# A retention layer and a GELU MLP: four first loads on other queues, a new load order, and seven half-size products in block 0

## The chip, the core and the metric

The kernel runs on one core of one Trainium2 chip. The metric is the device time of one execution in microseconds; the time before is the median of three runs. A profile is one execution recorded by the hardware profiler, and every duration in this document comes from such a record or from the runs' times.

## What is computed

Batch 8, 8 heads, 576 positions, head dimension 64; then an MLP of 512 to 2048 to 512 features over 8 x 576 = 4608 tokens, with the heads side by side as the 512 features.

```python
scores = q @ k.T / sqrt(64)                       # per batch and head
ret    = scores * gamma[h] ** (i - j)             # for i >= j, else 0; gamma = 1 - 2 ** (-5 - h)
x      = (ret @ v) -> [4608, 512]                 # heads side by side
h      = x @ w_in                                 # [4608, 2048]
g      = 0.5 * h * (1 + erf(h / sqrt(2)))
out    = g @ w_out                                # [4608, 512], float32
```

## The kernel before

**Attention, in units.** The 576 positions of a batch are four chunks of 128 and a tail of 64. A unit is one chunk of one batch (or the tails of two batches), 128 tokens, 36 units in all; units are taken in pairs of batches, and a group is the unit or the two units that are handled together. Units 0 to 3 are the first chunks of batches 0 to 3. For each group TensorE transposes q and k (`turn`, L407, tile `qk_ps`; from group 8 on VectorE does it, L430), multiplies them to scores (`scores`, tile `sc`), VectorE multiplies the scores by a decay mask (`masked`, L507, tile `ret`; `near` for the first chunks, `msk` and `mskp` later) and v by a decay (`scaled_v`, L516, tile `vh`), TensorE multiplies the two (`inner`, tile `o_ps`). What earlier chunks contribute runs through a state of 64 x 64 per head: `state` (L557 and L562, tile `u_ps`) adds a chunk's k and v products, VectorE and ScalarE keep it in `u_acc` and `u_sb` (L567 to L577), and `cross` (L613) applies it. `evacuate` (L636, or L373 and L375 for units 0 to 3) writes x in bf16; `dqT` is the decay that it applies, built up by POOL (L280) from one chunk to the next.

**MLP, in blocks.** Four units make a block of 512 tokens, nine blocks. The first product (`mlp1`, L656, tile `hT`) has weight `w_in`, in eight slices of 256 columns; ScalarE applies GELU into `g_all` (L661, L664). The second product of block 0 is plain (`mlp2`, L689, tile `oT`, 512 columns a matmul, ScalarE copies the sum out, L693). The second product of blocks 1 to 8, in halves p of 256 tokens, is done by seven half-size products instead of eight (`mlp2_fast`, L760, tiles `fa` and `fb`, 256 columns a matmul). They need four sums of `g_all` for each half (`g_sum`, L728), and once for the whole kernel eight sums of `w_out` (`w_out_sums`, L715, into `wt` and, the last two, into `w_out` itself). The order of the seven is 1 2 6 5 7 4 3; product 6 needs the second sum of `wt`, 7 the one written over `w_out`. Their results are put together by copies (L373, L375, tile `t`) and VectorE additions (`join`, L746). Blocks 6 to 8 do the first product in the same way (L865, L878).

**Loads.** q and k of unit 0 come over SyncE's and ScalarE's queues as fp32 (L114) and are cast by `either` (L373 on VectorE or L375 on ScalarE, whichever the planner takes to be free sooner). Everything else that is loaded early comes over POOL's queue, which casts to bf16 on the way: q, k, v of a unit (128 KB written each, L315; into the tile `early` for units 0 to 3), the slices of `w_in` (`wi0` to `wi7`, L270) and of `w_out` (`wo0` to `wo7`, L285), 256 KB written each. Their order is a list written out by hand:

```python
321      ORDER = ("wi0 io v0 k1 q1 v1 wi1 q2 k2 v2 wi2 k3 q3 v3 wi3 wi4 wi5 wi6 wi7 wo0 wo1 wo2 wo3 wo4 wo5 wo6 wo7 "
322               "q4 k4 q5 k5 v4 v5 dq2 q6 k6 q7 k7 v6 v7 q8 k8 q9 k9 v8 v9 dq3 q10 k10 v10 dq4 q11 k11 q12 k12 n11 n12 dq0").split()
```

`io` makes the index ramps and the constants that hang on them (`near`, `dv`, `dqT`), `dq2` is a POOL multiplication for `dqT`. Later v comes over SyncE's queue (L261), later q and k over POOL's in small pieces (L298, L305). At most eight POOL loads are under way at a time.

**What sets the order.** All instructions are issued by a planner in the kernel, which runs when the kernel is built: it keeps a clock for each engine (`T`), a landing time for each load (`land`, with `sw` for the time up to which POOL's queue is taken), and picks what to issue next by these; it also puts matmuls on zeros (tile `warm`, L1080 and L1107) where TensorE would wait in the first 16 us. Each engine then runs its own list in that order, and waits where an operand isn't there. `either` chooses engines by the same clocks. The pieces that the change touches:

```python
1032         if sum_due and sum_ready(*sum_due[0]) <= now + 0.1:
1033             t, p, _ = sum_due[0]
1034             jobs.append(((t + 0.5 * p - b2) * PER_B, lambda: g_sum(*sum_due.pop(0))))
1035         if wsum and (wsum[0][0] != "3" or not left(runs2, 0)):
1036             jobs.append(((FAST2[0] - b2) * PER_B, lambda: wsum.pop(0)[1]()))
...
1135         for key in u_due[:1]:
1136             if key != (1, 0) or nA >= 6:
1137                 acts.append((state_at(*key), "U"))
```

The first lets VectorE make the sums of g and of `w_out` when it has nothing more urgent; the last holds back the state product of units 2 and 3.

Of the kernel before, what the change touches and what calls it, by code (L numbers as in the profile page):

```python
# [9 lines left out]
FP32 = mybir.dt.float32  # L10
# [7 lines left out]
def kernel(  # L18
# [14 lines left out]
    nc = tc.nc  # L33
    ctx.enter_context(tc.manual_schedule())

    B, H, S, D = q.shape
# [5 lines left out]
    C = 128  # L42
    N_DM = d_model // 128
    N_DF = d_ff // 128
# [22 lines left out]
    FAST2 = tuple(range(1, N_BLK))  # L67
# [3 lines left out]
    N_QKT = 4  # L71
# [4 lines left out]
    ALLOW = 0  # L76
    AHEAD = 14
    RATE = 3.8
    HOT = 7.5
    SLACK, SB, PER_G, PER_B, TURN0 = 1.6, 9.0, 8.0, 40.0, 3.0  # L80
    FINE = 0.38
# [9 lines left out]
    tr_pool = ctx.enter_context(tc.tile_pool(name="tr", bufs=1))  # L91
# [8 lines left out]
    T = dict.fromkeys(("pe", "act", "dve", "pool", "sp"), 0.0)  # L100
# [10 lines left out]
    first = {}  # L111
    for nm, src, eng in (("q32", q, nc.sync), ("k32", k, nc.scalar)):
        t = first[nm] = o_pool.tile([128, H, D], FP32, tag="o_sb", name=nm)
        eng.dma_start(t, src[0, :, 0:C, :].rearrange("h s d -> s h d"))  # L114
    zeros = ld_pool.tile([128, 512], BF16, tag="v32", bufs=N_V32, name="zeros")
    nc.vector.memset(zeros, 0.0)
    lgh = const.tile([128, H, 1], FP32, name="lgh")
# [91 lines left out]
            on(engine, dur)  # L209


    sw = [0.0]
    turned = [0.0]
    flying = []
    dq_done = {1}
    land = {}
    loaded = {}
# [17 lines left out]
    def tiles_of(i):  # L235
        g = groups[group_of[i]]
        if i not in loaded:
            if i < 4:
                loaded[i] = (early_slice(2 * i, 2).rearrange("p (a h d) -> p a h d", a=2, h=H),
                             early_slice(8 + i, 1).rearrange("p (h d) -> p h d", h=H), None)  # L240
            else:
                n = group_of[i]
                if i != g[0]:
                    qk, kn = loaded[i - 1][0], loaded[i - 1][2]
                elif n not in BY_DVE:
                    qk = qk_tile("qk_ld").rearrange("p (a h j d) -> p a h j d", a=2, h=H, j=2)
                    kn = qk[:, 1]
                else:
                    qk = qk_tile("qkb_ld").rearrange("p (a f) -> p a f", a=2)
                    kn = ld_pool.tile([128, H, 2, D], BF16, tag="kn", bufs=N_KN, name="kn_ld") if len(g) > 1 else None  # L250
                loaded[i] = (qk, None if group_of[i] in BY_DVE else ld_pool.tile([128, H, D], BF16, tag="v", bufs=8, name="v_ld"), kn)
        return loaded[i]
# [12 lines left out]
    def load(what, i):  # L265
# [43 lines left out]
        for jj in (j,) if j is not None else range(2):  # L309
# [3 lines left out]
            else:  # L313
# [2 lines left out]
            land[what, i] = sw_dma(0.88, 0.9) if j is not None else sw_dma(0.68, 0.5)  # L316

    tiles_of(0)
    land["q", 0], land["k", 0] = 4.65, 5.2
    cast_due = {("q", 0): (loaded[0][0][:, 0], first["q32"]), ("k", 0): (loaded[0][0][:, 1], first["k32"])}  # L320
    ORDER = ("wi0 io v0 k1 q1 v1 wi1 q2 k2 v2 wi2 k3 q3 v3 wi3 wi4 wi5 wi6 wi7 wo0 wo1 wo2 wo3 wo4 wo5 wo6 wo7 "
             "q4 k4 q5 k5 v4 v5 dq2 q6 k6 q7 k7 v6 v7 q8 k8 q9 k9 v8 v9 dq3 q10 k10 v10 dq4 q11 k11 q12 k12 n11 n12 dq0").split()

    def next_order():
        item = ORDER.pop(0)
# [603 lines left out]
    for t in range(N_BLK):  # L929
        if t in FAST1:  # L930
            for i in range(4):
                runs1.append((t, [("h", t, i, x) for x in "1265743"]))
        elif t < 2:
            for lo, hi in zip((0, 256), (256, 512)) if t else ():
                runs1.append((t, [("1", t, m, 2, lo, hi) for m in range(0, N_DF, 2)]))
            if t == 0:
                runs1 += [(t, [("1", t, m, 2, lo, lo + 128) for lo in range(0, TOK, 128)]) for m in range(0, N_DF, 2)]
        else:
            runs1.append((t, [("1", t, m, 1, 0, TOK) for m in range(N_DF)]))
        if t in FAST2:  # L940
            for p in range(2):
                runs2.append((t, [("f", t, p, x) for x in "1265743"]))
        elif t == 0:
            runs2.append((t, [("2", t, ts, m, m + 2) for m in range(0, N_DF, 2) for ts in range(2)]))
            runs2.append((t, [("2", t, ts, m, m + 4) for ts in range(2, 4) for m in range(0, N_DF, 4)]))
        else:
            runs2.append((t, [("2", t, ts, m, m + 4) for ts in range(4) for m in range(0, N_DF, 4)]))
    waiting2 = {x for _, r in runs1 + runs2 for x in r}
# [3 lines left out]
    def left(runs, t):  # L952
        return sum(len(r) for u, r in runs if u == t)
# [39 lines left out]
        return x_ready(t, 0, TOK)  # L993

    sum_due = []
    for t in FAST2:
        for p in range(2):
            sum_due += [(t, p, i) for i in "1234"]

    def done_step(t, p, name):  # L1000
        return ("f", t, p, name) not in waiting2

    def sum_ready(t, p, i):
        if i != "3" and t > FAST2[0] and not done_step(t - 1, p, {"1": "5", "2": "6", "4": "3"}[i]):
            return 1e9
        return max(g_at.get((t, m, ts), 1e9) for m in range(N_DF) for ts in (2 * p, 2 * p + 1))

# [11 lines left out]
    def side_jobs(now):  # L1019

        jobs = []
        gA, gB = group_of[min(nA, N_U - 1)], group_of[min(nB, N_U - 1)]
        b1, b2 = at_block(runs1, n1), at_block(runs2, n2)
        idle = T["dve"] <= now + SLACK
        if nV < min(N_U, len(s_done) + N_VH) and land.get(("v", nV), 1e9) + 0.1 <= now and (nV < nA or nV >= VH_POOL):
            if idle if nV < VH_POOL else T["pool"] <= now + 0.5:
                jobs.append(((group_of[nV] - gB) * PER_G + 1.0 + 9.0 * (nV in raw), do_vh))
        if not idle:
            return jobs
        if nT in BY_DVE and nT < gB + N_QKT and all(land.get(("qk"[half], i), 1e9) + 0.1 <= now for i in groups[nT]):  # L1030
            jobs.append(((nT - gA) * PER_G + TURN0, do_turn))
        if sum_due and sum_ready(*sum_due[0]) <= now + 0.1:
            t, p, _ = sum_due[0]
            jobs.append(((t + 0.5 * p - b2) * PER_B, lambda: g_sum(*sum_due.pop(0))))
        if wsum and (wsum[0][0] != "3" or not left(runs2, 0)):
            jobs.append(((FAST2[0] - b2) * PER_B, lambda: wsum.pop(0)[1]()))
        if wsum1 and len(s_done) >= N_U - ALLOW:
            jobs.append(((FAST1[0] - b1) * PER_B, lambda: wsum1.pop(0)[1]()))
        if xsum_due and xsum_ready(*xsum_due[0]) <= now + 0.1:
            jobs.append(((xsum_due[0][0] - b1) * PER_B, lambda: x_sum(*xsum_due.pop(0))))  # L1040
        return jobs
# [42 lines left out]
    def attend(n):  # L1084
        nonlocal nB
        g = groups[n]
        for i in g:
            inner(i)
            nB += 1
        if u_due and state_at(*u_due[0]) <= T["pe"] + 0.2 and not (u_due[0] == (1, 0) and nA < 6):  # L1090
            state(*u_due[0])
        cross(n)
        for i in g:
            evacuate(i)
# [15 lines left out]
    while True:  # L1110
# [22 lines left out]
                ready = max(ready, u_ready.get((bp, ci - 1), 1e9))  # L1133
            acts.append((max(ready, free_time(out_banks(g))), "A"))
        for key in u_due[:1]:
            if key != (1, 0) or nA >= 6:
                acts.append((state_at(*key), "U"))
        if nA < N_U:
            n = group_of[nA]
# [93 lines left out]
```

## Time and profile before

| | |
|---|---|
| runs, us | 300.9, 300.47, 300.14; median 300.47 |
| the profiled execution, us | 300.81 |
| its span, first to last instruction, us | 298.9 |
| granted TensorE clock, mean | 0.996 |
| TensorE (PE) busy | 286.1 us, 96% |
| VectorE (DVE) busy | 226.7 us, 76% |
| ScalarE (ACT) busy | 135.1 us, 45% |
| POOL busy | 152.9 us, 51% |
| DMA, POOL's queue | 17.71 MB in 78048 packets |
| DMA, SyncE's and ScalarE's queues | 16.26 MB in 32992 packets and 0.26 MB in 1040 |

How to read it: busy time is the share of the span in which an engine has an instruction in it, PEld is the loading of matmul weights, which runs beside matmuls. The filler matmuls on zeros count as busy. Rows of the timeline merge instructions of the same kind that follow each other closely; a bracket behind a row gives the idle time of its engine before it and what ended it. A few matmul records are missing from a trace, so a count of 35 can stand for 36.

### The profile page before, as it was taken

How to read it: one execution, taken by the hardware profiler on the slowest of the kernel's cores; microseconds unless marked ns; L12 is line 12 of the kernel's file. 1: busy time of each engine (PE TensorE's matmuls, PEld its weight loads, DVE VectorE, ACT ScalarE, POOL GpSimd, SP SyncE). 2: the span in 40 equal slices, each digit the busy share in tenths (PEclk: the TensorE clock that was granted, in tenths of full speed). 3: DMA queues.
4: the chain of work that ended last, by engine and by line, in shares of the span. 5: the costliest groups of instructions: out<-in, count | busy, mean ns of one | idle time of the engine just before them, and what ended most of it. 6: DMA issues, size and time to landing. Idle time of an engine off the chain costs nothing.

```text
span 298.9 us, 8793 instructions
## 1 busy us (share of the span) xinstructions
PE 286.1 (96%) x3689; PEld 213.8 (72%) x3718; DVE 226.7 (76%) x432; ACT 135.1 (45%) x262; POOL 152.9 (51%) x232
## 2 busy tenths in 40 slices
PE   7899997999999999999998999999999999999994
PEld 2478555888657656667665666666888888888883
DVE  5762059999999889317969489756998999898751
ACT  7656225744343343542542434433554554546421
POOL 8976797899896899996986842000000000000000
PEclk9999999999999999999999999999999999999998
DMA  9999999999999999999979570201001101111014
GB/s 143 166 186 204 182 187 179 214 163 113 155 141 197 189 201 125 155 162 159 139 126 174 83 188 2 72 2 37 35 2 72 71 2 70 44 28 72 35 55 124
DMA packets 112119, 34.79 MB, mean 116 GB/s; under 512 B 89808, under 2 KB 107728, under 8 KB 112080
## 3 DMA queue, kind: packets, MB, share of 16 engines
q0 software_dynamic: 78048, 17.71, 66.8%
q1 hardware_dynamic: 32992, 16.26, 20.2%
q8 instruction: 29, 0.48, 0.7%
q10 hardware_dynamic: 1040, 0.26, 0.4%
q14 instruction: 10, 0.08, 0.1%
HBM read 42.47 MB, written 9.44 MB: 174 GB/s over the span
## 4 chain that ended last, share of the span: by engine, by line
PE 62%; DMA 16%; POOL 16%; issue 3%; DVE 1%; ACT 0%; POOLq 0%; DVEq 0%; ACTq 0%
PE fa L760 17%; PE hT L656 14%; PE fb L760 13%; PE ha L865 7%; PE hb L865 5%; POOL qkb_ld L298 5%; DMA qkb_ld<-in_q_dram 3%; DMA qk_ld<-in_q_dram 3%; POOL kn_ld L305 3%; DMA kn_ld<-in_k_dram 3%; DMA w_out<-in_moe_w_out_dram 3%; POOL early L315 3%; DMA qk_ld<-in_k_dram 3%; PE sc L462 2%; POOL w_in L270 2%
## 5 line engine op out<-in xcount | busy, mean ns | idle before, releaser
L656 PE MATMUL hT<-x,w_in 128*128 128x512 bf16 (+2 forms) x521 | 92.6, 314 | 3.1 <-DVE x L636 1.0
L656 PEld LDWEIGHTS <-w_in 128*128 128x128 bf16 x544 | 49.1, 98 | 26.1 <-issue 3.2
L661 ACT ACTIVATE g_all<-hT 128x512 bf16<-128x512 f32 x64 | 38.2, 597 | 49.8 <-PE hT L656 47.6
L760 PEld LDWEIGHTS <-g_all 128*128 128x128 bf16 x512 | 49.6, 98 | 11.0 <-issue 0.2
L760 PEld LDWEIGHTS <-s 128*128 128x128 bf16 x384 | 37.4, 98 | 8.9 <-issue 0.2
L746 DVE TENSOR_TENSOR o_sb<-fb,t 128x256 f32<-128x256 f32 x48 | 19.9, 417 | 25.4 <-ACT t L375 12.9
L870 ACT ACTIVATE g_all<-tt 128x512 bf16<-128x512 f32 x36 | 22.6, 630 | 29.4 <-DVE tt L878 29.3
L298 POOL DMA_DIRECT2D qkb_ld<-in_k_dram x56 | 30.9, 587 | 6.5 <-DMA kn_ld<-in_k_dram 4.7
L760 PE MATMUL fa<-w_out,g_all 128*128 128x256 bf16 x256 | 33.1, 273 | 0.0
L305 POOL DMA_DIRECT2D kn_ld<-in_k_dram x44 | 30.4, 731 | 5.2 <-PE u_ps L557 2.3
L298 POOL DMA_DIRECT2D qkb_ld<-in_q_dram x56 | 31.3, 599 | 2.2 <-DMA qkb_ld<-in_k_dram 1.2
L507 DVE TENSOR_TENSOR ret<-sc,mskp 128x512 bf16<-128x512 f32 x44 | 27.2, 677 | 3.2 <-PE sc L462 3.1
L878 DVE TENSOR_TENSOR tt<-hb,tt 128x512 f32<-128x512 f32 x36 | 24.5, 687 | 5.2 <-ACT tt L375 2.9
L664 ACT ACTIVATE g_all<-hT 128x512 bf16<-128x512 f32 (+1 forms) x36 | 19.2, 550 | 14.2 <-PE hT L656 14.1
L375 ACT COPY t<-fa 128x256 f32<-128x256 f32 x35 | 13.0, 371 | 19.6 <-PE fa L760 19.6
L636 DVE TENSOR_TENSOR x<-o_ps,dqT 128x512 bf16<-128x512 f32 (+1 forms) x36 | 20.9, 619 | 0.8 <-PE o_ps L613 0.6
L865 PEld LDWEIGHTS <-ws 128*128 128x128 bf16 x192 | 18.8, 98 | 2.2
L516 POOL TENSOR_TENSOR vh<-v,dvp 128x512 bf16<-128x512 f32 x14 | 15.1, 1134 | 5.2 <-DMA v<-in_v_dram 5.2
L430 DVE STREAM_TRANSPOSE qkT<-qkb_ld 128x512 f32<-128x512 f32 (+1 forms) x28 | 17.4, 637 | 0.0
L760 PE MATMUL fb<-w_out,g_all 128*128 128x256 bf16 x128 | 16.6, 273 | 0.0
L760 PE MATMUL fb<-w_out,s 128*128 128x256 bf16 x128 | 16.4, 273 | 0.1
L760 PE MATMUL fa<-wt,g_all 128*128 128x256 bf16 x128 | 16.4, 273 | 0.0
(123 smaller groups left out, 445.2 us busy)
## 6 DMA issues: line engine op xcount, KB each, us to landing
out_dram<-o_sb SPq DMA_DIRECT2D x31, 256.0 KB, 2.8
v<-in_v_dram SPq DMA_DIRECT2D x50, 128.0 KB, 4.7
qkb_ld<-in_q_dram POOLq DMA_DIRECT2D x44, 64.0 KB, 3.6
qkb_ld<-in_k_dram POOLq DMA_DIRECT2D x44, 64.0 KB, 3.8
kn_ld<-in_k_dram POOLq DMA_DIRECT2D x44, 64.0 KB, 4.5
w_in<-in_moe_w_in_dram POOLq DMA_DIRECT2D x8, 256.0 KB, 7.1
w_out<-in_moe_w_out_dram POOLq DMA_DIRECT2D x8, 256.0 KB, 9.8
out_dram<-o_sb SPq DMA_DIRECT2D x8, 128.0 KB, 2.4
```

Source lines behind the costliest of these rows:

```text
L298: nc.gpsimd.dma_start(qk[p0:p0 + 32, "qk".index(what), 0:HP * per].rearrange("p (h x) -> p h x", h=HP), {"q": q, "k": k}[what][2 * bp + jj ...
L305: nc.gpsimd.dma_start(kn[64 * e:64 * e + 64, :, j], k[2 * bp + j, :, ci * C + e:ci * C + C:2, :].rearrange("h s d -> s h d"))
L507: nc.vector.tensor_tensor(r, t, by, op=ALU.mult)
L636: nc.vector.tensor_tensor(x[:, :, n * y:n * y + n], o, dqT[:, :, ci * C:ci * C + n], op=ALU.mult)
L656: nc.tensor.matmul(hT[:, m - m0, :], lhsT=w_in[:, cc, m * 128:m * 128 + 128], rhs=x_tiles[t][:, cc, lo:hi], start=(cc == 0), stop=(cc == N ...
L661: nc.scalar.activation(g_all[:, t % 2, :, m0, :], hT.rearrange("p n (a c) -> p (n a) c", a=2), AF.Gelu)
L664: nc.scalar.activation(g_of(t, 2 * lo // TOK)[:, m0:m0 + n, lo_:lo_ + hi - lo], hT, AF.Gelu)
L746: nc.vector.tensor_tensor(dst, src, f[key], op=ALU.add)
L760: nc.tensor.matmul(dst, lhsT=x[:, kk, :], rhs=y[:, kk, :], start=(name in "125" and kk == 0), stop=(kk == HK - 1), skip_group_check=True)
L865: nc.tensor.matmul(dst[:, m, :], lhsT=a[:, cc, c0:c0 + 128], rhs=y[:, cc, :], start=(name in "125" and m == 0 and cc == 0), stop=(cc == HC ...
L870: nc.scalar.activation(g_of(t, part)[:, m0:m0 + 2], src, AF.Gelu)
L878: nc.vector.tensor_tensor(f[key], f["b"][1], f[key], op=ALU.add)
```

## The change

Four more first loads (q and k of unit 1, v of units 0 and 1) come over SyncE's and ScalarE's queues as fp32, into two tiles of the pool `tr`, and are cast like the first two. They are taken out of POOL's list, which gets another order: the loads of units 2 and 3 stand among the first slices of `w_in`, slices of `w_in` and `w_out` are mixed and not in the order of their numbers, and q4 comes before the last slice. The second half of block 0's second product (tokens 256 to 511) is done by the seven half-size products, with its four sums of g; the sums of `w_out` may be made from when the plain part of block 0 is done. The state product of units 2 and 3 is held back until 24 us of the planner's clock instead of until six units have their scores. The planner's landing times are set for the new loads.

```diff
+    STATE10 = 24.0
+    HW_AT = 5.9, 6.4, 6.9, 7.5
...
+    for nm, src, i, eng in (("q1", q, 1, nc.sync), ("k1", k, 1, nc.scalar), ("v0", v, 0, nc.sync), ("v1", v, 1, nc.scalar)):
+        if len(first) % 2 == 0:
+            t = tr_pool.tile([128, 2, H, D], FP32, tag="qkT", bufs=N_QKT, name="first")
+        first[nm] = t[:, len(first) % 2]
+        eng.dma_start(first[nm], src[i, :, 0:C, :].rearrange("h s d -> s h d"))
...
-    sw = [0.0]
+    sw = [7.0]
...
+    tiles_of(1)
     land["q", 0], land["k", 0] = 4.65, 5.2
-    cast_due = {("q", 0): (loaded[0][0][:, 0], first["q32"]), ("k", 0): (loaded[0][0][:, 1], first["k32"])}
-    ORDER = ("wi0 io v0 k1 q1 v1 wi1 q2 k2 v2 wi2 k3 q3 v3 wi3 wi4 wi5 wi6 wi7 wo0 wo1 wo2 wo3 wo4 wo5 wo6 wo7 "
-             "q4 k4 q5 k5 v4 v5 dq2 q6 k6 q7 k7 v6 v7 q8 k8 q9 k9 v8 v9 dq3 q10 k10 v10 dq4 q11 k11 q12 k12 n11 n12 dq0").split()
+    land["q", 1], land["k", 1], land["v", 0], land["v", 1] = HW_AT
+    cast_due = {("q", 0): (loaded[0][0][:, 0], first["q32"]), ("k", 0): (loaded[0][0][:, 1], first["k32"]),
+                ("q", 1): (loaded[1][0][:, 0], first["q1"]), ("k", 1): (loaded[1][0][:, 1], first["k1"]), ("v", 0): (loaded[0][1], first["v0"]), ("v", 1): (loaded[1][1], first["v1"])}
+    ORDER = ("q2 io k2 v2 wi1 wi2 q3 wi0 k3 wi4 wo0 v3 wi5 wo4 wi7 wi6 wo1 wo2 wi3 wo3 wo6 wo5 q4 wo7 q5 k4 k5 q6 "
+             "v5 q7 v4 k6 k7 k8 q8 q9 k9 v9 dq2 q10 v8 v7 v6 dq3 q11 n11 dq0 k10 v10 k12 k11 q12 n12 dq4").split()
...
         elif t == 0:
             runs2.append((t, [("2", t, ts, m, m + 2) for m in range(0, N_DF, 2) for ts in range(2)]))
-            runs2.append((t, [("2", t, ts, m, m + 4) for ts in range(2, 4) for m in range(0, N_DF, 4)]))
+            runs2.append((t, [("f", t, 1, x) for x in "1265743"]))
...
-    for t in FAST2:
-        for p in range(2):
+    for t in (0, *FAST2):
+        for p in range(2) if t else (1,):
             sum_due += [(t, p, i) for i in "1234"]
...
-        if i != "3" and t > FAST2[0] and not done_step(t - 1, p, {"1": "5", "2": "6", "4": "3"}[i]):
+        if i != "3" and t and not done_step(t - 1, p, {"1": "5", "2": "6", "4": "3"}[i]):
...
-        if wsum and (wsum[0][0] != "3" or not left(runs2, 0)):
-            jobs.append(((FAST2[0] - b2) * PER_B, lambda: wsum.pop(0)[1]()))
+        if wsum and (wsum[0][0] != "3" or not any(r and r[0][0] == "2" for _, r in runs2)):
+            jobs.append(((0.5 - b2) * PER_B, lambda: wsum.pop(0)[1]()))
...
-            if key != (1, 0) or nA >= 6:
+            if key != (1, 0) or now > STATE10:
```

How the planner places it, in the order of each engine's instructions: VectorE casts q1, k1 and v1 and ScalarE v0, all ahead of the first mask (`near`). TensorE has 11 filler matmuls instead of 22, 32 `oT` matmuls instead of 64, 56 more of the half-size kind; six of the `oT` matmuls stand among block 0's `hT`, the other 26 behind it. On VectorE the four sums of g and then the eight sums of `w_out` stand ahead of the first `msk` masks (units 4 and 5); before, the eight stood between the masks and x of units 4 to 9. TensorE's products of block 0's second half stand between transposes and scores of units 4 to 7, and ahead of block 1's `hT`. POOL's `dq2` comes after v9.

More of the change, by code (lines that the diff above doesn't have):

```diff
@@ L1089, in attend @@
             nB += 1
-        if u_due and state_at(*u_due[0]) <= T["pe"] + 0.2 and not (u_due[0] == (1, 0) and nA < 6):
+        if u_due and state_at(*u_due[0]) <= T["pe"] + 0.2 and not (u_due[0] == (1, 0) and T["pe"] <= STATE10):
             state(*u_due[0])
```

## Prediction

> **What bounds the kernel now.** First the page: span, busy line, slices.
>
> ```profile
> span 298.9 us, 8793 instructions
> ...
> PE 286.1 (96%) x3689; PEld 213.8 (72%) x3718; DVE 226.7 (76%) x432; ACT 135.1 (45%) x262; POOL 152.9 (51%) x232
> ...
> PE   7899997999999999999998999999999999999994
> DVE  5762059999999889317969489756998999898751
> ```
>
> A slice is 7.5 us. TensorE is full from the eighth (52 us) on, less so before. VectorE has a hole in slices 4 to 6, then nines. Next the busy time by stretch (start:end, length, PE, PEld, DVE, ACT, POOL, granted clock, DMA share, GB/s):
>
> ```profile
> 6.00:8.00 2.00, 1.73 (x19) 0.98 (x18) 1.58 (x7) 1.48 (x5) 2.00 (x4) 1.00 2.37 154
> 14.00:16.00 2.00, 1.84 (x36) 1.38 (x34) 1.07 (x2) 1.16 (x3) 2.00 (x4) 1.00 2.21 162
> 28.00:32.00 4.00, 3.95 (x48) 3.52 (x48) 0.00 (x0) 3.08 (x7) 2.77 (x4) 1.00 1.24 204
> 48.00:52.00 4.00, 3.04 (x56) 1.82 (x50) 4.00 (x8) 1.10 (x2) 2.78 (x5) 1.00 2.32 188
> ```
>
> About 155 GB/s move where q, k and v run in short rows, 205 where weight slices do: the loads are the limit of the first stretch. At 28 to 32 VectorE does nothing; at 48 to 52 it is full and TensorE is not. The timeline (start, length, instruction, idle before it) shows who waits:
>
> ```profile
> 9.61 0.40 PE L407 MATMUL qk_ps<-ident,early 128*128 128x128 bf16 x4 [0.58 <-DMA early<-in_q_dram]
> 20.12 2.37 PE L656 MATMUL hT<-x,w_in 128*128 128x256 bf16 x24 [0.38 <-DMA w_in<-in_moe_w_in_dram]
> 31.55 7.93 PE L689 MATMUL oT<-w_out,g_all 128*128 128x512 bf16 x35
> 39.74 1.09 DVE L373 COPY qkT<-qk_ps 128x512 bf16<-128x512 bf16 x3 [15.05 <-PE qk_ps L407]
> 41.77 2.48 DVE L507 TENSOR_TENSOR ret<-sc,msk 128x512 bf16<-128x512 f32 x4 [0.93 <-PE sc L480]
> 44.77 2.71 DVE L516 TENSOR_TENSOR vh<-v_ld,dv 128x512 bf16<-128x512 bf16 x2
> 47.41 1.28 DVE L715 TENSOR_TENSOR wt<-w_out 128x1024 bf16<-128x1024 bf16 x2
> 50.41 1.27 DVE L636 TENSOR_TENSOR x<-o_ps,dqT 128x512 bf16<-128x512 f32 x2
> 51.74 1.03 PE L656 MATMUL hT<-x,w_in 128*128 128x256 bf16 x8 [0.81 <-DVE x L636]
> ```
>
> Three stages: loads, until block 0's first product (hT) ends at 31.55; then block 0's second product (oT) beside two attention groups, until VectorE's x releases block 1's first product at 51.74; then TensorE, which alone is on the chain of waits from 107 us to its last rows, of which this is one (start, length, what):
>
> ```profile
> 289.35 3.49 PE fa L760 x32
> ```
>
> So a microsecond won before 51.74 should be kept, as long as later loads keep up.
>
> **Work taken off TensorE.** Thirty-two oT matmuls go (35 in 31.55 to 39.10, 0.216 each: 6.9) and 56 half-size ones come (3.49/32 = 0.109 each: 6.1): -0.8. Of hT, 16 of 256 columns become 32 of 128, the same columns: 0. Eleven of 22 filler matmuls on zeros go; they only fill waits: 0.
>
> **The loads.** Four 256 KB loads leave POOL for the SyncE and ScalarE queues. One q, k or v load costs 0.87 and a weight slice 1.29: POOL's issues (L315) from 26.43 on come 1.28 apart, one as each slice lands, and about 0.9 apart from 34.71. Landing is then 3.95 plus the sum of the loads before it: q1's 9.60 is 3.95 + five small + one slice; q2, by the same count 12.64, was waited for until 12.69. I assume that the DMA engines give a byte the same time from either queue. Before, they were fed by SyncE and ScalarE until about 4 us and by POOL after, without a gap, so the new queues bring no bytes, only another order. The Trainium skill says the same in "Trainium Kernel Development and Optimization", Key Constraints: issuing from several engines saves only issue time; by that rule the queue move by itself is worth nothing here, as in my sum.
>
> By the new order x of units 0 to 2 needs nine small loads first (11.8, the fp32 ones earlier, about 10), the first w_in slice lands at 13.1, and the last, w_in 3, twelve small loads and twelve slices on: 3.95 + 10.4 + 15.5 = 29.9. Its 16 products take 1.75, and I allow 0.5 for TensorE running behind, about its two waits shown above: hT ends at 32.2 (31.7 if it is not behind). That is 0.6 later than before; but six oT matmuls are done by then, and the last w_out slice lands at 35.9, before the last four oT need it at 37.0.
>
> The loads of units 4 to 7 come just in time: by the same count q5 lands at 36.8 for transposes at 37.8, k5 at 38.5 for 40.0, k7 at 43.7 for 44.5, v4 at 42.0 for a vh at 44.1. A load that is later than this margin (0.8 to 2) costs its excess one for one.
>
> The other instructions: ScalarE issues two more DMAs (0.49 each) ahead of its table load, so near ends 1.0 later, at 6.6, and the first mask, 7.77 before, comes later anyway. SyncE issues two; nothing is behind them until the first store at 38.8. Four casts come: q1, k1, v1 on VectorE ahead of the first mask, v0 on ScalarE, 0.43 to 0.58 each. The first mask thus waits for v1, near 10.2 instead of 7.77; hidden, because the first w_in slice is not there until 13.1.
>
> **Block 0's second half.** Four sums of g (L728, 0.68) and the eight sums of w_out (L715) now stand together on VectorE after the last gelu, in its hole, ahead of the first msk masks. VectorE starts such instructions 0.60 apart (41.77 to 44.17 for four). From hT's end: gelu 0.85 (33.05), four dependent sums 2.5 (35.55), eight 4.8 (40.35), a join and a copy 0.75 (41.1), scores to mask 0.6, four masks 2.4 (44.1), two vh, two joins, a copy 2.3 (46.4). TensorE meanwhile has 5.6 of oT, 6.1 of products, 1.8 of transposes and 0.5 of scores: 46.2 without a wait; o_ps, u_ps, u_acc and two x follow to 49.35. Block 1's first product starts there, 2.4 before 51.74. The state product of units 2 and 3 (STATE10; 32 small matmuls at 41.72 and VectorE's copy at 44.17) has moved into hT, off this chain; its 0.6 is part of the 2.4. TensorE has also done 16 transposes more by then (48 instead of 32; 16 take 0.9, 44.67 to 45.56): 3.3 ahead in all, which contains the -0.8.
>
> One charge: the two vh at 44.77 took 2.71 instead of 1.28, while POOL multiplied dqT at 45.83. One such multiplication (dq2), which fell in VectorE's hole, comes near 41 now. It costs 0 if it meets an instruction that reads PSUM (the masks at 52 kept 0.62 beside one) and 1.4 if it meets a sum or vh: I take 0.5. After 51.74 VectorE is 4.8 lighter up to 57, where TensorE's gaps add to 0.1: 0.
>
> Sum: 3.3 - 0.5 = 2.8. The profiled execution took 300.81 (span 298.9 plus 1.9), 0.3 above the median: 298.0 against it, 297.7 against 300.47.
>
> **Rivals.**
> *Loads ahead of the count.* If the two fp32 queues fill the start (246 GB/s at 2 to 4 us, against 154 later), all lands up to 1.0 earlier and dq2 misses: 2.8 + 1.0 + 0.5, 296.2.
>
> *The lead is lost to the fp32 loads.* For it: v in 128 KB pieces on SyncE took 4.7 to land beside POOL's loads, the first 256 KB q only 3.8 alone. If v1 lands at 12.5 instead of 10, masks, x and hT move 2.5: 0.3 is left, 300.2. "DMA: Bandwidth & Descriptors", Queues, rings and completion order, in the Trainium skill has each DMA engine go round-robin over the queues, by packets; no row here shows three queues at once, and by it v1 would land near 10.
>
> *Slower.* The same place, further on: nothing of VectorE passes the cast of v1. Gain is zero at a first mask at 13.0 (10.2 + 2.8); v1 landing at 13.8 with k2 and wi1 waiting behind it puts hT's end at 36 and costs 1.0: 301.5. Against it: both queues start at 0.74, before POOL's first packets.
>
> *A cold TensorE.* At the start 512-column fillers take 0.64 (seven in 4.45) and later 0.25 (six in 1.47), though the granted clock reads 1.00. With half the fillers gone TensorE could fall back near 10 us. The slow pace lasted some 5 us at the start; 5 us of it hold 2.5 of work, so 2.5 is lost, of which waits for loads take up 1.0: 1.5, 299.2. The Trainium skill's "TensorE: Matmul & The Clock Gate", What's actually happening, has such a fallback after an idle window; no wait in my count is that long.
>
> **Numbers.** Forecast 0.48, loads ahead 0.16, lead lost 0.16, cold 0.05, slower 0.15. A measurement here tells 0.3% (0.9 us) from nothing. Faster: forecast, loads ahead, cold and 0.03 of lead lost, 0.72; same 0.13; slower 0.15. Time 297.7; range 295.9 (loads ahead, with 0.3 for a lighter VectorE) to 300.5 (lead lost).
>
> **What would show it.** Right: w_in 3 landing near 30, hT of block 0 ending near 32, twelve sums on VectorE from 33 to 40, block 1's first product near 49.4, no new idle on TensorE after 60. Wrong: the cast of v1 waiting past 12; a gap on TensorE after oT for wt or qkT; transposes (L430) waiting for qkb_ld between 60 and 110, which would mean that TensorE's lead outran POOL's loads.

## The result: 0.8% slower

| | runs | median, us | ratio to before, 95% interval |
|---|---|---|---|
| before, same session | 4 | 300.34 (300.14 to 300.9) | |
| after | 4 | 302.62 (302.33 to 303.68) | 1.0079 (1.0051 to 1.0108) |

The forecast was 297.7 with a range of 295.9 to 300.5. Single executions scatter more in the later sessions (the kernel before took 298.9 to 303.65 in one of them), so verdicts below are ratios over 6 to 35 executions of a session; the profile of one kernel, `e10_plain`, fell into a disturbed execution and is not read.

The profiled execution took 302.59, span 300.8. Lines of the code are ten higher than before (L656 is L666). The page of the kernel after, span, busy line and slices of TensorE and VectorE:

```profile
span 300.8 us, 8906 instructions
...
PE 287.7 (96%) x3747; PEld 216.9 (72%) x3747; DVE 227.6 (76%) x439; ACT 138.3 (46%) x270; POOL 150.0 (50%) x228
...
PE   7679999999999999999998999999999999999994
DVE  5564097989998899426968559865998999899751
```

TensorE's seventh slice is full now, as the change means it to be; its second and third are emptier than before (7 6 7 for 7 8 9). The busy time by stretch shows where, in the columns of the prediction:

```profile
8.00:10.00 2.00, 1.90 (x20) 1.46 (x20) 0.80 (x3) 1.56 (x5) 1.28 (x2) 1.00 1.53 184
10.00:12.00 2.00, 0.21 (x3) 0.00 (x0) 0.00 (x0) 0.55 (x2) 0.00 (x0) 1.00 1.84 159
20.00:24.00 4.00, 2.73 (x42) 2.63 (x42) 0.42 (x1) 3.99 (x12) 1.65 (x3) 1.00 1.59 191
48.00:52.00 4.00, 3.98 (x46) 3.35 (x45) 3.63 (x8) 1.96 (x5) 4.00 (x4) 1.00 2.15 188
```

From 10 to 12 the engines all but stand (TensorE 0.21, ScalarE 0.55, the others 0); from 20 to 24 TensorE is short of work while ScalarE is full. At 48 to 52 TensorE is full, where before it had 3.04 of 4. The timeline names the waits:

```profile
12.11 0.61 PE L417 MATMUL qk_ps<-ident,early 128*128 128x128 bf16 x4 [1.89 <-DMA early<-in_k_dram]
12.37 0.43 DVE L383 CAST early<-first 128x512 bf16<-128x512 f32 x1 [3.43 <-DMA first<-in_v_dram]
13.05 1.28 DVE L517 TENSOR_TENSOR ret<-sc,near 128x512 bf16<-128x512 f32 x2
18.64 0.33 ACT L206 ACTIVATE dvp<-dvp,ln_scale 128x40 f32<-128x40 f32 x1 [3.05 <-DVE dvp L200]
18.98 1.28 ACT L207 ACT_TABLE_LOAD   x1
20.64 0.58 ACT L385 CAST x<-o_ps 128x512 bf16<-128x512 f32 x1
21.27 1.93 PE L666 MATMUL hT<-x,w_in 128*128 128x128 bf16 x24 [1.68 <-ACT x L385]
35.58 1.91 PE L666 MATMUL hT<-x,w_in 128*128 128x256 bf16 x16
47.15 2.48 DVE L517 TENSOR_TENSOR ret<-sc,msk 128x512 bf16<-128x512 f32 x4 [0.89 <-PE sc L490]
54.85 1.91 PE L666 MATMUL hT<-x,w_in 128*128 128x256 bf16 x16
```

VectorE waits 3.43 for v1, which lands at 12.35; the first mask starts at 13.05 instead of 7.77. Then ScalarE waits 3.05 for `dvp`, whose small VectorE instructions (17.84 to 18.61) stand behind three pairs of masks, loads a table, and only then casts x of unit 1, though its product `o_ps` was done at 17.8. From 21.27 on TensorE has no gap worth naming before 54.85.

Three landmarks split the time. Block 0's hT ends at 37.49 (35.58 + 1.91) instead of 31.72: 5.8 later. From there to block 1's first product it takes 17.36 instead of 20.02: 2.7 won. From that product to the end of the span 245.95 instead of 247.16: 1.2 won, of which the sixteen transposes done earlier can be 0.9. 5.8 - 2.7 - 1.2 = 1.9, the difference of the spans.

### The profile page after: what moved, and what is told of

Same layout as the page of the kernel before. It is cut to its first block, busy times and chain, and to the rows that moved or that the text cites. A ratio compares the mean times of both kernels' runs of the same rounds, so it can differ in the third digit from the quotient of the medians.

```text
span 300.8 us, 8906 instructions
## 1 busy us (share of the span) xinstructions
PE 287.7 (96%) x3747; PEld 216.9 (72%) x3747; DVE 227.6 (76%) x439; ACT 138.3 (46%) x270; POOL 150.0 (50%) x228
## 4 chain that ended last, share of the span: by engine, by line
PE 82%; DMA 6%; DVE 4%; POOL 4%; issue 1%; ACT 1%; DVEq 0%; POOLq 0%
PE hT L666 23%; PE fa L770 19%; PE fb L770 14%; PE ha L875 7%; PE hb L875 5%; DMA early<-in_k_dram 3%; PE sc L472 3%; PE o_ps L623 3%; PE o_ps L552 2%; PE oT L699 2%; DMA qk_ld<-in_k_dram 2%; DVE ret L517 2%; PE u_ps L567 1%; POOL kn_ld L312 1%; DMA qkb_ld<-in_q_dram 1%
## 5 line engine op out<-in xcount | busy, mean ns | idle before, releaser
L666 PE MATMUL hT<-x,w_in 128*128 128x512 bf16 (+2 forms) x560 | 94.0, 314 | 2.9 <-ACT x L385 1.7
L666 PEld LDWEIGHTS <-w_in 128*128 128x128 bf16 x560 | 50.3, 98 | 27.0 <-issue 3.8
L770 PEld LDWEIGHTS <-g_all 128*128 128x128 bf16 x544 | 52.6, 98 | 11.7 <-issue 0.7
L770 PEld LDWEIGHTS <-s 128*128 128x128 bf16 x408 | 39.1, 98 | 9.3 <-issue 1.2
L756 DVE TENSOR_TENSOR o_sb<-fb,t 128x256 f32<-128x256 f32 x51 | 21.3, 419 | 23.2 <-PE fb L770 12.8
L770 PE MATMUL fa<-w_out,g_all 128*128 128x256 bf16 x272 | 35.1, 273 | 0.0
L385 ACT COPY t<-fa 128x256 f32<-128x256 f32 x38 | 14.2, 373 | 26.2 <-PE fa L770 25.2
L770 PE MATMUL fa<-wt,s 128*128 128x256 bf16 x136 | 17.5, 273 | 0.2 <-DVE s L738 0.2
L770 PE MATMUL fb<-w_out,s 128*128 128x256 bf16 x136 | 17.5, 273 | 0.1
L770 PE MATMUL fa<-wt,g_all 128*128 128x256 bf16 x136 | 17.5, 273 | 0.1
## 6 DMA issues: line engine op xcount, KB each, us to landing
w_out<-in_moe_w_out_dram POOLq DMA_DIRECT2D x8, 256.0 KB, 10.2
```

The source lines that it names most:

```text
L666: nc.tensor.matmul(hT[:, m - m0, :], lhsT=w_in[:, cc, m * 128:m * 128 + 128], rhs=x_tiles[t][:, cc, lo:hi], start=(cc == 0), stop=(cc == N ...
L756: nc.vector.tensor_tensor(dst, src, f[key], op=ALU.add)
L770: nc.tensor.matmul(dst, lhsT=x[:, kk, :], rhs=y[:, kk, :], start=(name in "125" and kk == 0), stop=(kk == HK - 1), skip_group_check=True)
```

## Experiments

Each was timed in five rounds beside the kernel before. Landmarks are from one profiled execution each. "Stage 2" is the time from hT's end to block 1's first product. "Measured" gives medians over all executions; the ratios decide.

| kernel | first mask | hT of block 0 ends | block 1's first product | stage 2 | ratio to before, 95% interval |
|---|---|---|---|---|---|
| before | 7.77 | 31.72 | 51.74 | 20.02 | 1 |
| after | 13.05 | 37.49 | 54.85 | 17.36 | 1.0079 (1.0051 to 1.0108) |
| e1_loads | 12.61 | 37.05 | 55.34 | 18.29 | 1.0033 (1.0021 to 1.0044) |
| e2_products | 8.29 | 32.05 | 62.14 | 30.09 | 1.0179 (1.0151 to 1.0206) |
| e3_skew | 12.84 | 36.00 | 53.36 | 17.36 | 1.0027 (1.0007 to 1.0046) |
| e4_pool | 7.95 | 34.13 | 52.78 | 18.65 | 0.9994 (0.9971 to 1.0017) |
| e5_products_state | 7.95 | 32.44 | 50.96 | 18.52 | 1.0041 (1.0004 to 1.0078) |
| e6_pool_skew | 7.97 | 33.95 | 52.62 | 18.67 | 0.9988 (0.9956 to 1.0021) |
| e7_pool_k10 | 7.95 | 35.68 | 53.05 | 17.37 | 1.0020 (0.9989 to 1.0051) |
| e8_pool_skew_k10 | 7.97 | 33.39 | 51.99 | 18.60 | 0.9964 (0.9941 to 0.9987) |
| e9_hw_skew_k10 | 13.29 | 36.44 | 53.81 | 17.37 | 1.0033 (1.0001 to 1.0066) |
| e10_plain | | | | | 1.0065 (1.0035 to 1.0096) |
| e11_k6k7 | 7.95 | 33.68 | 52.32 | 18.64 | 1.0010 (0.9974 to 1.0047) |
| e12_two | 8.78 | 35.77 | 53.14 | 17.37 | 0.9999 (0.9963 to 1.0034) |

Behind block 1's first product the profiled executions (e2 and e10 aside) take 244.5 to 248.0 to the end of the span, in no order that follows the landmarks. So a landmark tells where a microsecond goes, not what the time will be.

**e1_loads: the loads alone.**

```diff
-            runs2.append((t, [("f", t, 1, x) for x in "1265743"]))
+            runs2.append((t, [("2", t, ts, m, m + 4) for ts in range(2, 4) for m in range(0, N_DF, 4)]))
...
-        if wsum and (wsum[0][0] != "3" or not any(r and r[0][0] == "2" for _, r in runs2)):
+        if wsum and (wsum[0][0] != "3" or not left(runs2, 0)):
```

> The loads alone: four loads over the SyncE and ScalarE queues and the new order of loads, with block 0's second half as before (plain oT products). Theory: the loads are what costs, and the seven products gain behind them what was reckoned. In the kernel after, hT of block 0 ended 5.8 later than before and block 1's first product began 3.1 later, so the second half gave back 2.7; without it 302.6 + 2.7 = 305.3, hT of block 0 ending at 37.3 as in the kernel after. Rival: the products gain nothing (the time after a late hT shrinks by itself, since VectorE has more done by then): 302.6, the same as after.

Measured 301.55 against 300.80. The loads alone reproduce the late hT (37.05, the same order on TensorE as in the kernel after up to there), so the loss is theirs; e1 keeps the new place of the state product, too. That the whole would be 2.7 worse without the products was wrong: block 1's first product moved by 0.5 only, and the end came out better than after. Stage 2 had already shrunk from 20.02 to 18.29 without the products, since the state product and some oT had moved ahead of hT's end (30.84, 26.36 and 34.71).

**e2_products: the products alone.**

```diff
-        if u_due and state_at(*u_due[0]) <= T["pe"] + 0.2 and not (u_due[0] == (1, 0) and T["pe"] <= STATE10):
+        if u_due and state_at(*u_due[0]) <= T["pe"] + 0.2 and not (u_due[0] == (1, 0) and nA < 6):
...
-            if key != (1, 0) or now > STATE10:
+            if key != (1, 0) or nA >= 6:
```

The four loads are back on POOL's queue, too, and the list of loads is that of the kernel before.

> The products alone: block 0's second half by seven half-size products with its twelve sums on VectorE, loads and their order as before. Theory: the second half gains what it gave back in the kernel after, 2.7: 297.6, with hT of block 0 ending at 31.6 and block 1's first product starting near 49. Rival: the twelve sums only find room on VectorE because the new order of loads and the other place of the state product made it; with the old ones block 1's first product stays at 51 to 52: 299.8 to 300.5.

Measured 305.89. Both missed. The planner lets the sums of `w_out` begin only when the states of units 0 to 3 are done; with `nA < 6` back, that is near 44.5, and the sums stand among the masks. TensorE waits 0.92, 0.94 and 1.37 between 43 and 47.4, and then this (busy time by stretch, the eighth figure is the granted clock):

```profile
44.00:46.00 2.00, 1.04 (x9) 0.78 (x8) 2.00 (x5) 0.76 (x2) 1.95 (x3) 0.71 1.75 222
46.00:48.00 2.00, 0.65 (x12) 0.51 (x14) 2.00 (x2) 1.79 (x4) 1.79 (x2) 0.50 1.74 159
48.00:50.00 2.00, 2.00 (x16) 1.34 (x13) 2.00 (x5) 0.00 (x0) 0.62 (x1) 0.50 2.37 155
```

The granted clock falls to half; eight matmuls of 256 columns take 1.89 (48.38) instead of 1.04. The products need the third part of the change, the state product inside hT.

**e3_skew: ScalarE's order.**

```diff
         make_args()
+        make_skewed()
...
         for hp in range(HP):
             make_dq(hp)
+        make_dvp()
...
-    later = [(6.4, "dve", 0.65, make_skewed), (7.3, "act", 1.8, make_dvp), (MSK_AT, "dve", 1.4, make_msk)]
+    later = [(6.4, "dve", 0.65, lambda: None), (7.3, "act", 1.8, lambda: None), (MSK_AT, "dve", 1.4, make_msk)]
```

> The kernel after, with one thing moved: VectorE's four small skew instructions and ScalarE's dvp and its table load for gelu (L200, L206, L207 of the kernel after) stand ahead of the casts and masks instead of behind three pairs of masks. Nothing else changes its place. Theory B (ScalarE's order): x of unit 1 waits 2.8 on ScalarE behind dvp, which waits for VectorE; without that it comes at 18.4 instead of 20.6, hT of block 0 ends about 2.2 earlier: 300.4. Theory A alone (late loads make the first mask late, and everything else follows): x of unit 1 would have come no sooner, 302.6. Cost at most 0.65 on VectorE ahead of the first casts, 303.2 if that is on the path.

Measured 301.96 against 300.80: 0.5% better than after by the ratios, 1.6 us. TensorE's 24 matmuls follow without the wait of 1.68:

```profile
19.76 1.94 PE L668 MATMUL hT<-x,w_in 128*128 128x128 bf16 x24
...
62.99 0.39 PE L419 MATMUL qk_ps<-ident,qk_ld 64*128 64x64 bf16 x8 [1.29 <-DMA qk_ld<-in_k_dram]
```

Theory B holds, though hT ends 1.5 earlier and not 2.2. The second line is new: a transpose of unit 10 waits 1.29 for its k, where the kernel after waited 0.22. Loads later on take back part of what is won.

**e4_pool: the queues undone, the order kept.**

```diff
-    for nm, src, i, eng in (("q1", q, 1, nc.sync), ("k1", k, 1, nc.scalar), ("v0", v, 0, nc.sync), ("v1", v, 1, nc.scalar)):
...
-    sw = [7.0]
+    sw = [0.0]
...
-    ORDER = ("q2 io k2 v2 wi1 wi2 q3 wi0 k3 wi4 wo0 v3 wi5 wo4 wi7 wi6 wo1 wo2 wi3 wo3 wo6 wo5 q4 wo7 q5 k4 k5 q6 "
+    ORDER = ("q1 io k1 v0 v1 q2 k2 v2 wi1 wi2 q3 wi0 k3 wi4 wo0 v3 wi5 wo4 wi7 wi6 wo1 wo2 wi3 wo3 wo6 wo5 q4 wo7 q5 k4 k5 q6 "
```

> The kernel after, with q1, k1, v0 and v1 back on POOL's queue, at the head of the same order; ScalarE and SyncE issue only q0 and k0 early. The planner places ScalarE's and VectorE's early instructions anew. Theory A (two fp32 queues beside POOL's slow all three): with one queue v1 lands near 9.2 and v2 near 11.8 instead of 12.35 and 12.84, the first mask comes near 10 instead of 13.05, hT of block 0 ends 32 to 34: 297.5 to 299.5. Theory C (the order of the loads costs, w_in 3 being last): hT of block 0 ends at 36 or later whatever the queue, 301.5 to 303.

Measured 300.93 against 300.80, ratio 0.9994: 0.85% better than after. v1 lands at 9.17, k2 at 10.97 and v2 at 11.80, in the order of issue; in the kernel after they land at 12.35, 12.06 and 12.84, together. The first mask starts at 7.95, since it no longer stands behind the cast of v1. The queue lines of the DMA view show the queues at work, first the kernel after at 9 to 11 (packets, MB, share; q0 is POOL's queue, q10 ScalarE's, q1 SyncE's):

```profile
q0 software_dynamic: 767, 0.10, 73.9%
q10 hardware_dynamic: 772, 0.20, 67.6%
q1 hardware_dynamic: 169, 0.04, 16.0%
```

and a kernel with POOL's queue alone, `e8_pool_skew_k10` at 5 to 7:

```profile
q0 software_dynamic: 2328, 0.29, 230.1%
```

A packet is one row of 64 numbers in either case (0.29 MB / 2328 = 125 bytes as bf16, 0.20 MB / 772 = 259 as fp32). In these two stretches POOL's queue alone moves 1164 rows per us, all queues together 854; over 4 to 10 it is 6678 rows in e4_pool and 5583 in the kernel after, 1113 and 931 per us. POOL's queue also starts later: in the kernel after it has no packet before 5.5, though its first load was issued at 1.25. At 9 to 11 POOL's and ScalarE's queues got the same number, 767 and 772, so there each load waits for the other's; from 6 to 7 the shares were not equal (POOL's 310, ScalarE's 547, SyncE's 42). The rule of the Trainium skill in "DMA: Bandwidth & Descriptors", Queues, rings and completion order, that an engine goes round-robin over the queues by packets, agrees with the counts at 9 to 11 and not with those at 6 to 7; what the prediction concluded from it, v1 near 10, did not come.

Theory A holds: hT ends 3.4 earlier (34.13) and the time falls by 2.5, though 300.9 is short of the 299.5 that it promised at most. Theory C, with hT's end at 36 or later whatever the queue, falls.

**e5_products_state: the products and the state product, with the old loads.** e2_products with STATE10 back in both conditions.

```diff
-        if u_due and state_at(*u_due[0]) <= T["pe"] + 0.2 and not (u_due[0] == (1, 0) and nA < 6):
+        if u_due and state_at(*u_due[0]) <= T["pe"] + 0.2 and not (u_due[0] == (1, 0) and T["pe"] <= STATE10):
...
-            if key != (1, 0) or nA >= 6:
+            if key != (1, 0) or now > STATE10:
```

> The products alone once more, with the third part of the change that the second half needs: the state product of units 2 and 3 moved into hT (STATE10), loads and their order as in the kernel before. In e2_products the sums of w_out waited for that state product and stood among the masks (45 to 53 us), TensorE idled and its granted clock fell to 0.50 there. Theory (the change's second half is worth what the kernel after showed behind its late hT, and only the loads undid it): the twelve sums stand together ahead of the first msk masks, no clock below 1.0; the stretch from 20 to 60 us loses 1.2 less than before and TensorE has 0.7 less work: 300.8 - 1.9 = 298.9, and 298.0 if the prediction's own 2.8 holds. Rival (an earlier start of block 1 meets loads of q and k that are not there): the gain is lost at transposes between 55 and 70, 300.5.

Measured 301.17 against 300.66. The sums stand together and the clock stays at 1.00, but block 1 starts only 0.8 earlier, and the rival's waits are there (timeline):

```profile
50.50 0.62 PE L408 MATMUL qk_ps<-ident,qk_ld 128*128 128x128 bf16 x8 [0.70 <-DMA qk_ld<-in_q_dram]
57.63 0.58 PE L408 MATMUL qk_ps<-ident,qk_ld 64*128 64x64 bf16 x8 [0.62 <-DMA qk_ld<-in_k_dram]
65.65 0.59 PE L463 MATMUL sc<-qkT 32*128 32x128 bf16 x20 [1.23 <-DVE qkT L431]
```

The last wait is for VectorE's transposes, which themselves wait for the k load (`kn_ld`) at 63.7 and 64.9. TensorE had 0.8 more in hand and met loads that were no earlier.

**e6, e7, e8: the early win, the late k load, and both.** On e4_pool; e6 with the edit of e3_skew, e7 with this, e8 with both:

```diff
-             "v5 q7 v4 k6 k7 k8 q8 q9 k9 v9 dq2 q10 v8 v7 v6 dq3 q11 n11 dq0 k10 v10 k12 k11 q12 n12 dq4").split()
+             "v5 q7 v4 k6 k7 k8 q8 q9 k9 v9 dq2 q10 v8 v7 v6 k10 v10 dq3 q11 n11 dq0 k12 k11 q12 n12 dq4").split()
```

> e4_pool with the skew instructions and ScalarE's dvp and table load early, as in e3_skew. In e4_pool x of unit 1 still waited 1.4 on ScalarE; this takes that away, so hT of block 0 ends about 1.4 earlier (near 32.5). Theory (the late k load of unit 10, issued at 55 and landed at 62.4, sets the time at which TensorE may go on at 62.5, whatever came before): time the same as e4_pool, 300.9, with the wait for qk_ld grown from 1.4 to near 2.8. Rival (a microsecond won early is kept, as the prediction has it): 299.5.

> e4_pool with two loads moved in the order: k10 and v10 stand right behind v6, ahead of dq3, q11, n11 and dq0, as they did in the kernel before. Theory (the late k10 costs 1.4 at 62 us): the wait for qk_ld there goes, 300.9 - 1.4 = 299.5. Rival (the loads as a whole are late there, so that another one is waited for instead): 300.9.

> Both edits, of e6_pool_skew and of e7_pool_k10, at once. If the early win of 1.4 is lost at k10 and k10 itself costs 1.4, the two together gain 2.8 where the first alone gains nothing: 298.1. If the loads as a whole limit the stretch up to 65 us: 299.5 to 300.9.

Measured 300.16, 301.32 and 299.58 against 300.66. e6 gained nothing that can be told, as its theory said, but not at unit 10: the wait for x was gone and hT still ended only 0.2 earlier, because its last slice was not there:

```profile
32.03 1.92 PE L661 MATMUL hT<-x,w_in 128*128 128x256 bf16 x16 [0.73 <-DMA w_in<-in_moe_w_in_dram]
```

w_in 3 landed at 31.98. The wait at unit 10 did not grow (1.1). In e7 the wait at unit 10 is gone, and nothing was won. Its profiled execution lost 1.6 up to hT's end to a fall of the granted clock (last section), in a stretch where its program is that of e4, and waited 2.2 for a join at 155, which e4's did not. Only both together are faster than before, by 0.36%, interval 0.13 to 0.59; that is 1.1 us, the expectation's second branch (299.5 to 300.9) and not its first (298.1). That it takes both is not shown: in 7 of e6's 12 executions the mean granted clock was 0.997 or more and their median is 299.81, beside 299.58 for e8, whose 12 were all at 0.997 or more; in e6's other five it was 0.993 or 0.994 and the median is 302.35. In e8 the next wait stands in stage 2:

```profile
46.11 0.41 DVE L751 TENSOR_TENSOR o_sb<-fb,t 128x256 f32<-128x256 f32 x1
...
46.61 0.61 PE L412 MATMUL qk_ps<-ident,qk_ld 128*128 128x128 bf16 x8 [1.25 <-DVE o_sb L751]
```

The line blames VectorE's join, which ended at 46.52. But k7 landed at 46.48; either could be it.

**e11_k6k7: which of the two.** e8 with k6 and k7 ahead of v5 and v4.

```diff
-             "v5 q7 v4 k6 k7 k8 q8 q9 k9 v9 dq2 q10 v8 v7 v6 k10 v10 dq3 q11 n11 dq0 k12 k11 q12 n12 dq4").split()
+             "k6 q7 k7 v4 v5 k8 q8 q9 k9 v9 dq2 q10 v8 v7 v6 k10 v10 dq3 q11 n11 dq0 k12 k11 q12 n12 dq4").split()
```

> e8_pool_skew_k10 with k6 and k7 ahead of v5 and v4 in the order of loads (q6 k6 q7 k7 v4 v5). In e8_pool_skew_k10 the transposes of unit 7 waited 1.4 at 45 to 46.6; k7 lands at 46.5 to 47.3 in all kernels with the new order of loads, 2.8 later than the prediction's ledger had it. Theory (that load sets the time): the wait goes, 299.6 - 1.4 = 298.2. Rival (VectorE sets it: four masks, a vh and two joins stand one behind the other from 43.6 to 47, and the transposes wait for the bank that the join empties): 299.6, the wait unchanged.

The transposes did not wait (44.62). But the planner also put them one product earlier in TensorE's list, ahead of that join, so this run does not tell the load from the join. Nor do the others: the join ended at 47.24, 47.12 and 46.52 in e4, e6 and e8, and k7 landed at 47.27, 47.11 and 46.48. Either alone would have held the transposes as long. The time did not follow: ratio 1.0010. The last of v4 and v5 now lands at 47.0, x comes later, and the wait is one step on:

```profile
52.32 1.03 PE L661 MATMUL hT<-x,w_in 128*128 128x256 bf16 x8 [1.06 <-DVE x L641]
```

Block 1's first product comes at 52.3, in e8 at 52.0. This order did not help; no other was tried.

**e9_hw_skew_k10 and e12_two: the queues again, four loads and two, with both mends.** e9 is e3_skew with the order of e7; e12 is e9 with v0 and v1 on POOL's queue (`"v0 io v1 q2 k2 v2 ..."`).

> The kernel after with the two mends of e8_pool_skew_k10 (skew and dvp early, k10 and v10 behind v6), and the four loads still as fp32 over the SyncE and ScalarE queues. Against e8_pool_skew_k10 (0.9964 of before) it differs in the queues of four loads alone. Theory A (three queues at once bring the four fp32 loads and POOL's k2 and v2 down together at 11 to 13, where POOL's queue alone has v1 at 9.2): the first mask comes near 13, lag of TensorE at 20 us about 3 more than in e8_pool_skew_k10; of that 1.5 to 2.5 stays: 301.0 to 302.0. Rival (dvp's wait and k10 were all that the queues cost): 299.6.

> Half of the queue move: q1 and k1 as fp32 over SyncE and ScalarE, v0 and v1 on POOL's queue at the head of the order, with the mends of e8_pool_skew_k10. Theory A (the queues share the DMA engines by packets, so what is issued together lands together): two loads delay POOL's first by about their own time, v1 lands near 9 to 10, first mask near 10.5; time between e8_pool_skew_k10 and e9_hw_skew_k10, nearer the first: 299.6 to 300.3. Rival (any use of a second queue beside POOL's costs its packet rate): as e9_hw_skew_k10, 301 to 302. Rival (the early queues help as the change means them to, and four were too many): 298.5 to 299.2.

None, two and four loads on the fp32 queues give 0.9964, 0.9999 and 1.0033. The outer intervals (0.9941 to 0.9987, 1.0001 to 1.0066) do not meet, so the move of four loads, with the casts and the planner's new times that come with it, costs 0.7%, 2.1 us. The same step without the edit of k10, e3 against e6, is 1.0027 against 0.9988: 0.4%, 1.2 us, with intervals that meet. Two loads stand between, with an interval too wide to say more. (e9's landmarks are those of its shortest execution, 300.04 against a median of 302.40.)

e12 also shows that an early first mask is not enough. v1 landed at 9.84, as expected, and the mask started at 8.78, but TensorE then waited 1.59 for q2 on POOL's queue (10.74) and 1.16 for x of unit 1, and hT ended at 35.77, nearer to e9 (36.44) than to e8 (33.39).

The rule of the Trainium skill in "Trainium Kernel Development and Optimization", Key Constraints, that several issuing engines save only issue time, was read in the prediction as a cost of zero. The measurement decides: here the move of four loads to a second kind of queue beside POOL's cost time.

**e10_plain: what the products are worth at the end.** e8 with block 0's second half plain (the edit of e1_loads).

> e8_pool_skew_k10 with block 0's second half as plain oT products again: no seven products, and the sums of w_out later, as in the kernel before. Theory (the products gain 0.8 of TensorE's work and some 0.5 in the stretch, as the time from hT's end to block 1's first product shows between e1_loads and the kernel after: 18.3 against 17.4): 0.9 to 1.3 slower than e8_pool_skew_k10, 300.5 to 300.9. Rival (the products cost more later, by VectorE's twelve sums and joins, than they save: e1_loads stood at 1.0033 of before where the kernel after stood at 1.0079, e5_products_state at 1.0041 where before stands at 1): 1.2 faster, 298.4.

Measured 303.16 against 301.23. Here the products gain 1% (1.0065 against 0.9964); between e1_loads and after they lose 0.46%, between before and e5 0.41%. Up to block 1's first product the products' share in a pair is below 1 us (18.29 against 17.36 in stage 2). What differs more lies far behind: between 140 and 180 TensorE has a single wait of 1.0 in the kernel before, 1.2 in the one after, 1.0 in e1_loads, 2.4 in e11_k6k7 and only 0.2 in e8, at another instruction in most. The planner lays out everything behind an edit anew. What the products are worth at the end stays open.

## Why the prediction was wrong

**Work taken off TensorE (-0.8).** Eight products of 256 columns start 0.87 to 0.88 after the eight before (43.38, 44.26): 0.109 each, as reckoned. Right, and too small to decide.

**The loads.** This is the step that failed: "I assume that the DMA engines give a byte the same time from either queue", and with it that the fp32 loads would be there first, near 10, and "the first mask thus waits for v1, near 10.2 ... hidden". v1 landed at 12.35 and the first mask started at 13.05. The ledger lets loads land one after the other at 0.87, nine small ones by 11.8. But these nine stood three each in three queues that ran at once, so the last of each queue landed near the end of the nine: k2 at 12.06, v1 at 12.35, v2 at 12.84. With equal shares that alone puts v1 near 11.8 and not near 10 (an estimate from the ledger's own count). And the nine were slower together: v2, the last, came at 12.84 where POOL's queue alone had it at 11.80, as in the ledger.

The rival of the lost lead had v1 at 12.5 and the slower one put the point of no gain at a first mask of 13.0; they were given 0.16 and 0.15, and their places were right. Their prices were not: the first still had 0.3 to gain and the second 301.5, where the kernel took 302.62. The queue step costs 2.5 (after against e4), 1.2 (e3 against e6) or 2.1 (e9 against e8).

**What stands behind the first mask.** "Hidden, because the first w_in slice is not there until 13.1" named one operand and not ScalarE's list. x of unit 1 needs ScalarE past `dvp`, which needs VectorE past three pairs of masks. e3 puts this at 1.6. The order of instructions showed it before the run.

**hT's end at 32.2.** It came 5.3 later, and block 1's first product 5.5 later than forecast, so nearly all was lost here. Without the queue move hT ends at 34.13 (e4), without the wait for `dvp` as well at 33.95 and 33.39 (e6, e8); 1.2 to 1.8 stay. The ledger drifts: w_in 3 was put at 29.9 and landed at 32.44 after, and at 31.4 to 32.2 in e4, e6 and e8, with POOL's queue alone; k7 was put at 43.7 and landed at 46.48 after and at 46.5 to 47.3 in these three. In them hT ends at 33.4 to 34.1. The mended kernel e8 (0.9964, 299.3 on 300.34) still lacks 1.6 to 297.7; that these late loads are the 1.6 is argued from e8's waits for a slice of w_in (0.70 at 23.55) and at the transposes of k7 (1.25), not shown by a run.

**Block 0's second half, 17.15 from hT's end.** 17.36 to 17.37 in five kernels (after, e3, e7, e9, e12). Right, in part by luck: it holds only where hT ends at 35.7 or later. Where it ends at 33.4 to 34.1, TensorE waits 1.25 to 1.32 at the transposes of k7 (e4, e6, e8), and it is 18.6 to 18.7. The step "TensorE ... 46.2 without a wait" held, as far as the traces tell, because the late hT had given the loads time.

**The charge of 0.5 for dq2.** No sum or vh ran long (four sums of `w_out` in 2.49, vh 0.68): 0.

**A microsecond won before 51.74 is kept.** Of 3.1 lost at block 1's first product, 0.9 are the transposes and 1.9 came out at the end: about right for a loss. For a gain it does not hold: e5 came 0.8 earlier and met late loads at 57 and 65. The condition was written down ("as long as later loads keep up"), with its sign ("transposes waiting between 60 and 110"); it was not priced.

**Cold TensorE.** It came, in small: after the wait of 1.89 scores of 128 columns take 0.61 (13.19) where e8 at the same time takes 0.40, and hT's first eight 1.06 (16.38) where the next take 0.62 (18.41). Useful matmuls from 12.1 to 17.4 took about 1.6 longer (0.22 for transposes, 0.42 for scores, 0.50 for `o_ps`, 0.44 for hT), at most, since masks paced much of this stretch. It is part of what the queue step costs.

## What to carry to other kernels

Price a load that moves to a second queue by the rows of all queues that run at that time, and take the last loads of queues that run at once to land together, near the end of the group: an early consumer loses even where no byte is added. Follow an engine's list behind each late operand to the end; an instruction that nobody is waiting for (a table, a constant) is a wall if its own operand comes late. And before a gain is counted as kept, compare the new time of need with the landing times of the next stage's loads: here the early gains of e3, e5 and e6 each met one that was not there.

## What the runs showed of the hardware

**The granted clock fell after a wait of 1.96, and after two shorter ones.** e4_pool and e7_pool_k10 have the same program here. In e4's profiled execution 24 matmuls follow a wait of 1.38, in e7's the same 24, at the same time, a wait of 1.96, because TensorE had begun the matmuls before at 13.80 and not at 14.38 (timelines):

```profile
18.57 1.93 PE L659 MATMUL hT<-x,w_in 128*128 128x128 bf16 x24 [1.38 <-ACT x L378]
```

```profile
18.57 3.52 PE L659 MATMUL hT<-x,w_in 128*128 128x128 bf16 x24 [1.96 <-ACT x L378]
```

The second ran at a granted clock of 0.50 (20 to 22). In the kernel after a wait of 1.68 at the same place did not do it. In e2_products the clock fell between 44 and 46 after two waits of 0.92 and 0.94 with 0.61 of work between them, so the length of one wait does not decide. The Trainium skill, "TensorE: Matmul & The Clock Gate", What's actually happening, gives an idle window of some 3.4 us for the fall; here a wait of 1.96, with TensorE busy for 0.61 of the 2 us around its start, was enough. In 8 of 12 executions of either kernel the mean granted clock was 0.991 to 0.994 (e7's profiled one 0.992, e4's 0.999), so e4 probably fell as often; no trace shows where.

**Half speed with a granted clock of 1.00.** The doubled times at 12 to 17 in the kernel after stand beside a clock of 1.00 in every stretch, so the clock's row does not show that case; the mean time of one matmul does.

**ScalarE is held by its own DMA issues.** Its two further issues were counted at 0.49 each; they took 0.73 and 1.82 (the last from 2.02 to 3.84), and the table load waited for them. Nothing on the path depended on it here.
